# Column-tiled dense groups, row-norm applications on GpSimd, and a later back transposition in a fused attention and token-MLP block

## Chip, cores and metric

The kernel runs on one core of a Trainium2 chip. The metric is device time in microseconds of one execution; the time before is the median of three runs, 292.4 us (292.23 to 293.14). Engines are named as the profile names them: PE is TensorE (PEld its weight loads), DVE VectorE, ACT ScalarE, POOL GpSimd, SP the queue that issues the DMAs.

## What is computed

The reference, cut to what matters (S = 2048 tokens, D = 512, H = 32 heads of 16, window 256, F = 1792):

```python
mod = (silu(c) @ w_mod)            # sa, ca, ga, sb, cb, gb: one row of 512 each
h = layernorm(x) * (1 + ca) + sa
q, k, v = split_heads(h @ wqkv)
scores = q k^T / 4, masked to 0 <= i - j < 256
x = x + ga * (softmax(scores) v) @ wo
h = layernorm(x) * (1 + cb) + sb
h = layernorm(h)                    # the MLP's own norm
u = gelu(h^T @ w1 + b1)             # mixes tokens: contracts S, gives (D, F)
x = x + gb * (u @ w2 + b2)^T
```

The second norm is thus two norms in a row for each token: norm, scale and shift, norm.

## The kernel before

The 2048 tokens are 16 blocks of 128 rows, in four row groups (tg) of four blocks. A short preamble normalises row group 0, makes its first q, k and v, and the modulation rows. Then come two stages.

**The attention stage** is a loop over 80 units: four row groups x four head sets of eight heads (g8) x five kinds of unit (k). In the text, unit u is 20 tg + 5 g8 + k, and "ul" is its number within the row group. Units k = 0, 2, 3, 4 work on "A" scores, k = 1 on "C" scores (the window's diagonal triangles, in 64 x 64 pieces). In each unit the program writes, in this order: the exp of the unit's first score tile (L526), the scores of the next unit (L477 and masks L485, or L504 and L513), in k = 1 and k = 4 the closing of a head set's parity (last value products L557, then the DVE transposition of `po` into `t2`, L583), the matmuls of at most one dense group, the second exp, the queued DVE and POOL work, the evacuation of the dense group, and the value products of the unit before (L537 of A units, L557 of C units).

A dense group is four accumulating matmuls of 128 x 128 weights with 512 columns: v (L250), q or k (L270), a modulation row broadcast (L297), the output projection `wo` (L330) or half of a part of the MLP's first product (L659). `plan(tg)` writes out by hand in which unit each group stands. All use PSUM tile `dn`, which has one buffer; `po`, the accumulator of the value products, also has one; scores have three. Scores run in 32 x 128 and 32 x 64 array tiles, value products in 128 x 32 and 64 x 32, dense groups on the whole 128 x 128 array. A q group's evacuation is the cast to QT (L282), a k group's the cast to ks (L285) on DVE and two masked copies KT (L288) on POOL, v's the cast into VaugT (L261), wo's the residual add into x (L338).

Other work goes through a small planner. `dve` is a list of chains; each chain is a list of steps (function, cost, gap), and `run_dve(u, budget)` lets steps go while their costs fit the unit's budget; after a step its chain rests for `gap` units. The budget comes from a running estimate of DVE's load. Engines run their queues in the order in which the program wrote them, so a step that waits holds what stands behind it on its engine. The chains:

- `norm_rest`: `quotient` (reciprocal zr on DVE, L591; product `merge` on POOL, L592), then `back` (transposition into OTd on DVE, L599), which `wo` reads. It is put ahead of all other chains.
- `ln1_apply`: four normalisations (xn, L218) of the next row group, in units 2 and 3 of a row group.
- `ln23(tb)` for the 12 blocks whose `wo` lies in the loop: `p1` statistics of x on DVE (L608, L610) and rstd on POOL (an add L198 and a pow L202); `p2` application on DVE (L614), then scale and shift on POOL (L625, L626); `p3` statistics of h2 and rstd; `p4` application (L614) into `hb`.

**The MLP stage** contracts `hb` with w1 (L819, L906) and the result with w2 (L926), nearly all on PE; the last four blocks get their output projection (L841) and second norm inside it.

Of the kernel before, what the change touches and what calls it, by code (L numbers as in the profile page):

```python
# [8 lines left out]
DT = mybir.dt  # L9
ACT = mybir.ActivationFunctionType  # L10
ALU = mybir.AluOpType
# [17 lines left out]
def kernel(  # L29
# [25 lines left out]
    dma = nc.sync  # L55

    const = ctx.enter_context(tc.tile_pool(name="const", bufs=1))
    small = ctx.enter_context(tc.tile_pool(name="small", bufs=4))
    xpool = ctx.enter_context(tc.tile_pool(name="xpool", bufs=1))
    xres = [xpool.tile([P, D], DT.bfloat16, name=f"x{t}") for t in range(NT)]  # L60

# [106 lines left out]
    epool = tc.alloc_tile_pool(name="epool", bufs=6)  # L168
    cpool = tc.alloc_tile_pool(name="cpool", bufs=4)
    npool = tc.alloc_tile_pool(name="npool", bufs=2)  # L170
    NG = NT // 4
    QT = [[None] * ND for _ in range(NG)]
    KeT = [[None] * ND for _ in range(NG)]
# [50 lines left out]
    def transpose_group(tg, pair, pool):  # L224
# [18 lines left out]
                )  # L243
        return mms, evac, 1.2

    def v_group(tg, tl, pool, act=False):
        def mms():
            pv = pool.tile([P, D], DT.float32, name="dn")
            for dc in range(ND):
                nc.tensor.matmul(  # L250
                    pv[:], lhsT=h1T[tg][:, dc, tl * P : (tl + 1) * P],
                    rhs=wqkv[:, dc, 2 * D : 3 * D], start=(dc == 0), stop=(dc == ND - 1),
                )
            return pv

        def evac(pv):
            o, i = VaugT[tg][:, tl, :, 0:DH], pv[:].rearrange("p (h d) -> p h d", d=DH)
            if act:
                nc.scalar.activation(out=o, in_=i, func=ACT.Copy)
            else:  # L260
                nc.vector.tensor_copy(out=o, in_=i)  # L261
        return mms, evac, 0.0 if act else 0.7

    def qk_group(tg, g8, kind, pool, act=False):
        col0 = g8 * P + (D if kind == "k" else 0)

        def mms():
            pq = pool.tile([P, 4 * P], DT.float32, name="dn")
            for dc in range(ND):
                nc.tensor.matmul(  # L270
                    pq[:], lhsT=wqkv[:, dc, col0 : col0 + P], rhs=h1T[tg][:, dc, :],
                    start=(dc == 0), stop=(dc == ND - 1),
                )
            return pq
# [18 lines left out]
    def bc_group(v, dst, add1, pool):  # L293
        def mms():
            ps_b = pool.tile([P, D], DT.float32, name="dn")
            for k in range(ND):
                nc.tensor.matmul(  # L297
                    ps_b[:], lhsT=sT_rep[:, k, :], rhs=wmod[:, k, v * D : (v + 1) * D],
                    start=(k == 0), stop=(k == ND - 1),
                )  # L300
            return ps_b

        def evac(ps_b):
            if add1:
                nc.vector.tensor_scalar_add(out=dst[:], in0=ps_b[:], scalar1=1.0)
            else:
                nc.vector.tensor_copy(out=dst[:], in_=ps_b[:])
        return mms, evac, 0.7
# [14 lines left out]
    def wo_group(tb, pool):  # L323
        tg, tl = divmod(tb, 4)

        def mms():
            assert len(folded) == ND
            pa = pool.tile([P, D], DT.float32, name="dn")
            for g in range(ND):
                nc.tensor.matmul(  # L330
                    pa[:], lhsT=OTd[tg][g][:, tl * P : (tl + 1) * P], rhs=wod[:, g, :],
                    start=(g == 0), stop=(g == ND - 1),
                )
            return pa

        def evac(pa):

            nc.vector.tensor_tensor(out=xres[tb][:], in0=pa[:], in1=xres[tb][:], op=ALU.add)  # L338
        return mms, evac, 0.7
# [20 lines left out]
    with tc.manual_schedule():  # L360
# [224 lines left out]
        def norm_rest(tg, g8):  # L585
# [11 lines left out]
            def back():  # L597
                OTd[tg][g8] = opool.tile([P, 4 * P], DT.bfloat16, name=f"OTd{g8}")
                nc.vector.transpose(out=OTd[tg][g8][:], in_=m[:])  # L599
            return [(quotient, 0.4, 1), (back, 0.7, 0)]  # L600


        def ln23(tb):
# [7 lines left out]
                v[key + "r"] = rstd_of(v[key][:, 1:2], 1, "ln2")  # L611

            def apply(out, src, key):
                nc.vector.tensor_scalar(  # L614
                    out=out, in0=src, scalar1=v[key][:, 0:1], scalar2=v[key + "r"][:],
                    op0=ALU.subtract, op1=ALU.mult,
                )
# [2 lines left out]
                stats(xres[tb][:], "m2")  # L620

            def p2():
                v["h2"] = npool.tile([P, D], DT.bfloat16, name="h2")
                apply(v["h2"][:], xres[tb][:], "m2")
                nc.gpsimd.tensor_tensor(out=v["h2"][:], in0=v["h2"][:], in1=bc_cb1[:], op=ALU.mult)  # L625
                nc.gpsimd.tensor_tensor(out=v["h2"][:], in0=v["h2"][:], in1=bc_sb[:], op=ALU.add)  # L626

            def p3():
                stats(v["h2"][:], "m3")

            def p4():
                done.add(tb)
                apply(hb[tb][:], v["h2"][:], "m3")
            return [(p1, 0.9, 2), (p2, 0.45, 2), (p3, 0.9, 2), (p4, 0.45, 0)]

        dve = []

        def add_dve(u, ps):
            dve.append([list(ps), u])

        def run_dve(u, budget):
            spent = 0.0
            for chain in dve:
                while chain[0] and chain[1] <= u and spent + chain[0][0][1] <= budget:
                    f, cost, gap = chain[0].pop(0)
                    f()
                    spent += cost
                    chain[1] = u + gap
# [4 lines left out]
        def part_group(fc, k):  # L653
            def mms():
# [1 line left out]
                if k == 0:  # L656
                    part[fc, "ps"] = ps_dn.tile([P, D], DT.float32, name="dn")
                for sc in range(4 * k, 4 * k + 4):
                    nc.tensor.matmul(  # L659
                        part[fc, "ps"][:], lhsT=w1box["a"][:, sc, fc * P : (fc + 1) * P], rhs=hb[sc][:],  # L660
                        start=(sc == 0), stop=(sc == 7),
                    )
                return part[fc, "ps"]
# [112 lines left out]
            u += 1  # L776

    ps_s.release()
    npool.release()
    cpool.release()  # L780
    epool.release()
# [189 lines left out]
```

## Time and profile before

| | |
|---|---|
| median of 3 runs | 292.4 us |
| the profiled execution | 294.43 us, of it span 292.7 us |
| attention stage (first exp to the first L819) | 16.5 to 194.45 us |
| first MLP product (L819, L906; with the last output projections) | 194.45 to 240.4 us |
| second MLP product and output | 240.4 to 292.7 us |
| busy in 108 to 151 us (43.0 us) | PE 37.14, ACT 38.08, DVE 33.01, POOL 25.75 us |

The stages can be told apart in the chain of waits, since L819, L906 and L926 stand in it as three long pieces. A row of a group tells line, engine, operation, output and input tiles, shape, count; then busy time in all and the mean of one in ns; then the idle time of that engine ahead of these instructions and what ended it. A row of a timeline has the start and the length in us, and in brackets the wait ahead of it and what ended it. The profile's matmuls are pipelined: a single one lasts 0.38 us from start to end, but they start 0.216 us apart, so matmul costs are read from starts.

### The profile page before, as it was taken

What the parts mean: (1) busy time and instruction counts of PE and PEld (TensorE: products, weight loads), DVE (VectorE), ACT (ScalarE), POOL (GpSimd) and SP (SyncE); (2) the same over time, 40 slices, a digit from 0 to 9 for tenths busy, and PEclk for the clock granted to TensorE, in tenths of its full rate; (3) what the DMA queues carried; (4) which work ended last, traced back from release to release, by engine and by line L of the source; (5) the groups of instructions that cost most, each with busy time, mean ns of one, the idle gap of its engine ahead of it and who ended that gap; (6) DMA issues with size and microseconds to landing.
All of it is one profiled execution on the core that took longest, in us unless ns stands there. A gap on an engine that the chain in (4) does not pass through costs nothing.

```text
span 292.7 us, 11229 instructions
## 1 busy us (share of the span) xinstructions
PE 261.8 (89%) x5096; PEld 132.7 (45%) x5096; DVE 170.5 (58%) x358; ACT 170.5 (58%) x192; POOL 99.4 (34%) x163
## 2 busy tenths in 40 slices
PE   7877898998988887898986898999999999999994
PEld 2533454444455454454443454544444444444441
DVE  6464685664778768778667667888902100505253
ACT  7468687897898987989978889923008220000000
POOL 5020423311437634765538556594400000000000
PEclk9799999999999999999979999999999999999999
DMA  6976000069100000000000000089940000012031
GB/s 198 360 238 214 4 2 3 4 226 404 69 4 4 2 4 3 3 4 4 2 4 2 2 4 4 2 287 411 421 203 3 0 0 0 20 55 72 0 110 36
DMA packets 15380, 24.85 MB, mean 85 GB/s; under 512 B 2276, under 2 KB 11492, under 8 KB 15332
## 3 DMA queue, kind: packets, MB, share of 16 engines
q1 hardware_dynamic: 15332, 24.13, 23.1%
q8 instruction: 40, 0.66, 0.9%
q14 instruction: 8, 0.07, 0.1%
HBM read 22.03 MB, written 2.10 MB: 82 GB/s over the span
## 4 chain that ended last, share of the span: by engine, by line
PE 71%; DVE 16%; POOL 6%; ACT 4%; issue 2%; DVEq 0%; POOLq 0%
PE py L926 17%; PE dn L270 8%; PE pu L819 7%; PE pu L906 7%; PE po L537 5%; PE pss L504 4%; PE dn L250 4%; PE pss L477 4%; PE po L557 4%; DVE t L583 4%; PE dn L330 3%; POOL merge L592 3%; PE dn L659 2%; ACT VaugT L381 2%; DVE zr L591 2%
## 5 line engine op out<-in xcount | busy, mean ns | idle before, releaser
L526 ACT ACTIVATE et<-pss 128x1024 bf16<-128x1024 f32 (+1 forms) x160 | 147.1, 980 | 26.3 <-PE pss L485 17.9
L926 PE MATMUL py<-guT,w2r 128*128 128x512 bf16 x224 | 48.5, 379 | 0.0
L270 PE MATMUL dn<-h1T,wqkv 128*128 128x512 bf16 x128 | 33.2, 384 | 4.3 <-DVE h1T L240 1.5
L933 DVE SCALAR_TENSOR_TENSOR o<-py,bFM,bc_gb 128x512 bf16<-128x512 f32 x16 | 11.4, 746 | 43.9 <-PE py L926 43.9
L477 PE MATMUL pss<-QT,KT 32*128 32x192 bf16 (+2 forms) x704 | 26.4, 239 | 8.8 <-ACT et L526 4.7
L926 PEld LDWEIGHTS <-w2r 128*128 128x128 bf16 x224 | 21.9, 98 | 26.4
L592 POOL TENSOR_TENSOR merge<-t,zr 128x512 bf16<-128x512 f32 x16 | 17.0, 1061 | 38.7 <-DVE zr L591 38.7
L583 DVE STREAM_TRANSPOSE t<-po 128x512 f32<-128x512 f32 x32 | 22.9, 717 | 12.3 <-PE po L557 12.3
L537 PE MATMUL po<-et,VaugT 128*32 128x192 bf16 (+2 forms) x704 | 25.2, 244 | 2.4 <-DVE t L583 2.4
L202 POOL TENSOR_TENSOR ln_rstd<-ln_ve,mhalf 128x1 f32<-128x1 f32 (+1 forms) x40 | 24.0, 600 | 3.3
L198 POOL TENSOR_SCALAR ln_ve<-ln_mv 128x1 f32<-128x1 f32 (+1 forms) x40 | 9.8, 244 | 44.5 <-DVE ln_mv L212 21.4
L537 PEld LDWEIGHTS <-VaugT 128*32 128x32 bf16 x704 | 11.6, 95 | 27.4 <-issue 26.7
L477 PEld LDWEIGHTS <-KT 32*128 32x128 bf16 x704 | 11.6, 92 | 19.1 <-issue 13.1
L557 PE MATMUL po<-et,VaugT 64*32 64x64 bf16 x960 | 19.0, 193 | 1.3 <-DVE VaugT L261 1.2
L485 PE MATMUL pss<-mask_q,mask_k 32*128 32x64 bf16 (+1 forms) x736 | 18.3, 197 | 0.0
L250 PE MATMUL dn<-wqkv,h1T 128*128 128x512 bf16 x64 | 17.2, 396 | 0.7 <-DVE ks L285 0.5
L270 PEld LDWEIGHTS <-wqkv 128*128 128x128 bf16 x128 | 10.7, 98 | 15.4 <-issue 4.6
L282 DVE CAST QT<-dn 128x512 bf16<-128x512 f32 x15 | 10.3, 687 | 12.4 <-PE dn L270 8.5
L288 POOL TENSOR_SCALAR KT<-ks,mask_even 128x512 bf16<-128x512 bf16 x14 | 9.7, 694 | 21.1 <-DVE ks L285 21.1
L504 PE MATMUL pss<-QT,KT 32*64 32x64 bf16 x1024 | 14.8, 195 | 1.4 <-issue 1.3
L557 PEld LDWEIGHTS <-VaugT 64*32 64x32 bf16 x960 | 11.0, 92 | 10.6 <-issue 4.8
L485 PEld LDWEIGHTS <-mask_k 32*128 32x128 bf16 x736 | 15.6, 94 | 0.3
(112 smaller groups left out, 358.6 us busy)
## 6 DMA issues: line engine op xcount, KB each, us to landing
w2r<-in_B_w_dram SPq DMA_DIRECT2D x14, 512.0 KB, 9.9
w1a<-in_B_w_dram SPq DMA_DIRECT2D x11, 448.0 KB, 7.7
wmod<-in_w_mod_dram SPq DMA_DIRECT2D x6, 512.0 KB, 4.9
w1b<-in_B_w_dram SPq DMA_DIRECT2D x5, 448.0 KB, 6.5
x<-in_A_x_dram SPq DMA_DIRECT2D x16, 128.0 KB, 2.7
out_dram<-otile SPq DMA_DIRECT2D x16, 128.0 KB, 1.7
wqkv<-in_A_wqkv_dram SPq DMA_DIRECT2D x2, 384.0 KB, 6.2
wqkv<-in_A_wqkv_dram SPq DMA_DIRECT2D x1, 512.0 KB, 6.1
```

The source lines that it names most:

```text
L202: nc.gpsimd.tensor_tensor(out=r[:], in0=ve[:], in1=mhalf[:, 0:n], op=ALU.pow)
L250: nc.tensor.matmul(pv[:], lhsT=h1T[tg][:, dc, tl * P : (tl + 1) * P], rhs=wqkv[:, dc, 2 * D : 3 * D], start=(dc == 0), stop=(dc == ND - 1),)
L270: nc.tensor.matmul(pq[:], lhsT=wqkv[:, dc, col0 : col0 + P], rhs=h1T[tg][:, dc, :], start=(dc == 0), stop=(dc == ND - 1),)
L477: nc.tensor.matmul(pss[j // 2][:, j % 2, c0 : c0 + nq], lhsT=keys(kb, g8, par)[rows[j], k0 : k0 + P], rhs=QT[tg][g8][rows[j], q0 : q0 + nq ...
L485: nc.tensor.matmul(pss[j // 2][:, j % 2, c0 : c0 + 64 * nb].rearrange("p (b q) -> p b q", q=64), lhsT=mask_k[rows[j], P * what : P * what ...
L504: nc.tensor.matmul(pss[a][64 * half : 64 * half + 64, j % 2, c0 : c0 + 64], lhsT=keys(kb, g8, par)[rows[j], k0 : k0 + 64], rhs=QT[tg][g8][ ...
L526: act = nc.scalar.activation(out=et[:, :, 0:n], in_=state.pop((u, a))[:, :, 0:n], func=ACT.Exp, scale=SCORE_SCALE,)
L537: nc.tensor.matmul(state["po"][32 * j : 32 * j + 32, q0 : q0 + nq], lhsT=VaugT[kb // 4][:, kb % 4, 8 * g8 + 2 * j + par, :], rhs=state["e" ...
L557: mm = nc.tensor.matmul(state["po"][32 * j : 32 * j + 32, q0 : q0 + 64], lhsT=VaugT[kb // 4][part64, kb % 4, 8 * g8 + 2 * j + par, :], rhs ...
L583: nc.vector.transpose(out=state["t2"][:, par, :], in_=state["po"][:])
L592: nc.gpsimd.tensor_tensor(out=m[:].rearrange("p (b a d) -> p a b d", a=2, d=DH), in0=t2v[:, :, :, 0:DH], in1=zr[:].to_broadcast([P, 2, 16, ...
L926: nc.tensor.matmul(pys[tl][:], lhsT=w2r[:, fc, tb * P : (tb + 1) * P], rhs=guT[fc][:], start=(fc == 0), stop=(fc == NF - 1),)
```

## The change

It has four parts.

1. Dense groups: each 128 x 128 by 512 matmul of v, q/k, broadcast, `wo` and part groups becomes four matmuls of 128 x 32 weights, each in its own column tile of the array, with the same moving operand, into 32 partitions of the same PSUM tile.
2. `ln23`: both applications (`p2`, `p4`) go from DVE to POOL; `p2` now stands directly behind `p1`, `p4` behind `p3`, with three units between `p2` and `p3`; their planner costs become 0.0.
3. `back` rests two units behind `quotient` instead of one.
4. h2 gets its own pool of three buffers, `small` has six instead of four, and `p2` is let go only while fewer than three rows are between `p2` and `p4`.

```diff
-    small = ctx.enter_context(tc.tile_pool(name="small", bufs=4))
+    small = ctx.enter_context(tc.tile_pool(name="small", bufs=6))
...
+    lnpool = tc.alloc_tile_pool(name="lnpool", bufs=3)
...
+    def dense(out, lhsT, rhs, start, stop):
+
+        for j in range(4):
+            cols = slice(32 * j, 32 * j + 32)
+            nc.tensor.matmul(
+                out[cols, :], lhsT=lhsT[:, cols], rhs=rhs, start=start, stop=stop,
+                tile_position=(0, 32 * j), skip_group_check=True,
+            )
+
     def v_group(tg, tl, pool, act=False):
         def mms():
             pv = pool.tile([P, D], DT.float32, name="dn")
             for dc in range(ND):
-                nc.tensor.matmul(
-                    pv[:], lhsT=h1T[tg][:, dc, tl * P : (tl + 1) * P],
+                dense(
+                    pv, lhsT=h1T[tg][:, dc, tl * P : (tl + 1) * P],
                     rhs=wqkv[:, dc, 2 * D : 3 * D], start=(dc == 0), stop=(dc == ND - 1),
                 )
...
-            return [(quotient, 0.4, 1), (back, 0.7, 0)]
+            return [(quotient, 0.4, 2), (back, 0.7, 0)]
...
             def apply(out, src, key):
-                nc.vector.tensor_scalar(
+                nc.gpsimd.tensor_scalar(
...
             def p2():
-                v["h2"] = npool.tile([P, D], DT.bfloat16, name="h2")
-                apply(v["h2"][:], xres[tb][:], "m2")
-                nc.gpsimd.tensor_tensor(out=v["h2"][:], in0=v["h2"][:], in1=bc_cb1[:], op=ALU.mult)
-                nc.gpsimd.tensor_tensor(out=v["h2"][:], in0=v["h2"][:], in1=bc_sb[:], op=ALU.add)
+                live.add(tb)
+                h2 = v["h2"] = lnpool.tile([P, D], DT.bfloat16, name="h2")
+                apply(h2[:], xres[tb][:], "m2")
+                nc.gpsimd.tensor_tensor(out=h2[:], in0=h2[:], in1=bc_cb1[:], op=ALU.mult)
+                nc.gpsimd.tensor_tensor(out=h2[:], in0=h2[:], in1=bc_sb[:], op=ALU.add)
...
             def p4():
                 done.add(tb)
+                live.discard(tb)
                 apply(hb[tb][:], v["h2"][:], "m3")
-            return [(p1, 0.9, 2), (p2, 0.45, 2), (p3, 0.9, 2), (p4, 0.45, 0)]
+            return [(p1, 0.9, 0), (p2, 0.0, 3, lambda: len(live) < 3), (p3, 0.9, 0), (p4, 0.0, 0)]
...
                 while chain[0] and chain[1] <= u and spent + chain[0][0][1] <= budget:
-                    f, cost, gap = chain[0].pop(0)
+                    if not all(free() for free in chain[0][0][3:]):
+                        break
+                    f, cost, gap = chain[0].pop(0)[:3]
```

The q/k, broadcast, `wo` and part groups call `dense` in the same way as the v group.

## The prediction

> **What bounds the kernel now.** I read the page first, then the groups by form, the chain of waits, the timeline of three stretches, and PE's waits in the attention stage.
>
> ```profile
> span 292.7 us, 11229 instructions
> PE 261.8 (89%) x5096; PEld 132.7 (45%) x5096; DVE 170.5 (58%) x358; ACT 170.5 (58%) x192; POOL 99.4 (34%) x163
> PE 71%; DVE 16%; POOL 6%; ACT 4%; issue 2%; DVEq 0%; POOLq 0%
> ```
>
> ```profile
> 240.38 48.36 PE py L926 x224
> ```
>
> The page's head and its chain by engine; then a row of the chain in order of time (start, length). From 194.45 us on PE runs without a gap (the chain's last rows before the output are PE alone), and the change leaves that half as it is. The attention stage, 16.5 to 194.45 us, is a loop of 80 units. I call T(u) the start of unit u's first exp (L526). ACT starts its two exps 0.92 us apart, so a unit can't be under 1.84 us. Where the chain passes through C scores (k=0) and a dense group it takes 2.30. So PE sets about three units of five, ACT the other two, and stalls come on top. A stall, read from the timeline around unit 44:
>
> ```profile
> 108.85 1.06 POOL L592 TENSOR_TENSOR merge<-t,zr 128x512 bf16<-128x512 f32 x1 [3.19 <-DVE zr L591]
> 109.94 0.71 DVE L599 STREAM_TRANSPOSE OTd<-merge 128x512 bf16<-128x512 bf16 x1 [0.35 <-POOL merge L592]
> 110.58 2.47 DVE L218 TENSOR_SCALAR xn<-x,ln_mv,ln_rstd 128x512 bf16<-128x512 bf16 x4
> 111.10 1.16 POOL L626 TENSOR_TENSOR h<-h,bc_sb 128x512 bf16<-128x512 bf16 x1
> 112.98 0.68 DVE L282 CAST QT<-dn 128x512 bf16<-128x512 f32 x1
> 113.80 0.40 PE L477 MATMUL pss<-QT,KT 32*128 32x256 bf16 x12 [1.46 <-DVE QT L282]
> ```
>
> DVE waits for POOL's merge, everything behind it on DVE is late, the evacuation of QT is last, and PE's next scores start 1.46 us late. So the value of each edit lies in what DVE has to wait for, and POOL is who it waits for.
>
> **Column tiles.** A dense matmul alone costs 48.36/224 = 0.216 us. Behind one, PE starts the next one of its own shape 0.216 us later, but the first L537 0.309 us later (median over the trace): 0.093 us to change the array's shape. Here it shows as four matmuls from 136.28 to 137.24, 0.96 where 4 x 0.216 is 0.86:
>
> ```profile
> 136.28 1.04 PE L330 MATMUL dn<-wod,OTd 128*128 128x512 bf16 x4
> 137.24 0.41 PE L537 MATMUL po<-et,VaugT 128*32 128x256 bf16 x12
> 137.58 0.30 PE L557 MATMUL po<-et,VaugT 64*32 64x64 bf16 x16
> ```
>
> The same lines price the new shape. The 12 L537 matmuls are three pieces of 512 columns in all, in four column tiles, and take 0.34 us with a shape change in them. One after another they would take four times 0.21. So four column tiles stream side by side at full rate, and a dense group keeps its 0.86 us. It becomes L537's shape, so the change behind it goes: 56 groups are followed by L537, 56 x 0.093 = 5.2 us, of which only units with k=0, 1, 4 (and most of row group 0, whose exps are shorter) lie on the path. The change of shape ahead of a dense group stays. 864 extra matmul and load pairs are hidden: in L537 they start 3 to 4 ns apart.
>
> The Trainium skill, TensorE: Matmul & The Clock Gate, Part 3 (The mechanism), says a weight load overlaps running matmuls only where the row group differs; here all four column tiles have the same rows. That would make a rival, priced below. The trace speaks against it: L537 pieces of 64 columns follow each other in 0.03 us with four loads between.
>
> **Applications on POOL.** 24 tensor_scalar leave DVE (L614, 0.46 and 0.41 us, 10.4 in all; DVE is not full, so this counts only where an evacuation stands behind). The trace has no such application on POOL. The nearest row is L288, the same operation and shape with one tensor input, 0.695; the lower bound is the 128x1 tensor_scalar of L198, 0.24, the upper the two-input L625, 1.157. I take 0.70 (one tensor input).
>
> ```profile
> L202 POOL TENSOR_TENSOR ln_rstd<-ln_ve,mhalf 128x1 f32<-128x1 f32 x32 | 18.3, 573 | 2.7
> L592 POOL TENSOR_TENSOR merge<-t,zr 128x512 bf16<-128x512 f32 x16 | 17.0, 1061 | 38.7 <-DVE zr L591 38.7
> L625 POOL TENSOR_TENSOR h<-h,bc_cb 128x512 bf16<-128x512 bf16 x12 | 13.9, 1157 | 4.3 <-DVE h L614 4.3
> L288 POOL TENSOR_SCALAR KT<-ks,mask_even 128x512 bf16<-128x512 bf16 x14 | 9.7, 694 | 21.1 <-DVE ks L285 21.1
> ```
>
> With the 0.08 us between dependent POOL instructions, p1 and p2 of a row are ve 0.30, pow 0.64, apply 0.78, mul 1.24, add 1.11: 4.07 us in one block. p3 and p4 are 0.30 + 0.64 + 0.66 = 1.6. The row takes 5.7 us of POOL against 4.2 before.
>
> **The order.** The planner counts p2 and p4 as 0.0 and lets p1 and p2 go in one unit, so rows come in bursts. Following its budgets unit by unit through the code gives: rows 0, 1 in units 31, 32; 2, 3 in 37, 39; 4, 5, 6 in 49, 50, 51; 7 in 57; 8, 9, 10, 11 in 69, 70, 71, 72. Every merge goes to POOL behind these blocks, and every `back` waits for its merge on DVE, with evacuations (and the transposition of po) behind it; `dn` and `po` have one buffer, so PE then waits too. The second unit of grace (about 2.1 us) is less than one block of 4.07.
>
> At nothing I cost: the larger pools (`small`, `lnpool`; the gate of three rows in flight takes the place of a wait for a buffer); OTd one unit later (`wo` reads it in unit 7 of the next row group, `back` is then in unit 3; were it five units late, `wo` would stand in PE's queue); hb from POOL (rows 0 to 7 are done by unit 60, the parts read them from unit 72; rows 8 to 11 are read after 202 us). No DMA moves.
>
> **The sum**, stage by stage. T is from the exps of the trace. Within a unit I place the steps where the trace has them (the closing's transposition 2.2 to 2.5 us after T, the evacuation of the dense group about 3.4 after), move them later only by the waits that I name, and let each engine take its queue in order with the durations above:
>
> - Units 0 to 31: 20 on-path groups x 0.093 = 1.9, some of it where DVE ends the wait anyway: -1.4.
> - Units 31 to 45 (31.26 us now). POOL starts 4.5 us after T(31) and isn't idle before merge[1,3]: four rows 16.3, three p3+p4 4.8, two merges 2.1, two KT pairs 2.8, ending at 30.5. The three xn now ahead of `back` meet these blocks; an xn beside L626 took 1.31 instead of 0.40. For each the bounds are 0 and 1.16; I take 0.8 in all: merge at 31.3. Behind it on DVE: back 0.71, xn 0.40, QT 0.69, then scores: T(45) at 33.8, +2.5.
> - Units 45 to 69 (54.7 now). merge[2,1] behind rows 4 and 5, and merge[2,2] behind row 6 and three p3+p4, hold DVE by 1.7 us each: +1.1 for units 45 to 61 with the shape changes off. Units 61 to 68 then hold no row work, and their present stalls (1.17 and 1.29 us at L557 and L477, POOL's rows 6 and 7 ahead of an evacuation, and 1.4 in unit 61, where the granted clock was 0.5 for 3.4 us) go: 20.1 to 16.0. Together -3.0.
> - Unit 69 to the MLP (25.3 now, 169.13 to 194.45). POOL starts row 8 at 3.4: four rows 16.3, three p3+p4 4.8, two merges 2.1, so merge[3,2] ends at 26.7. Then back 0.71, transposition of po 0.72, the last value products 1.2: the MLP starts at 29.4, +4.1. Ahead of that p3[11] waits for row 11 until 22.4.
> - MLP: 0. The last `back` lands beside the 2.7 us of L819 that cover it now; without that cover it costs 1 us.
>
> Sum: -1.4 + 2.5 - 3.0 + 4.1 = +2.2 us. The profiled execution took 294.43 (span 292.7 and 1.7 around it), which would become 296.6; the runs' median is 292.4, 2.0 below the profiled one, so 294.6. About 0.3%, 0.9 us, is what a measurement here can tell from no change.
>
> The Trainium skill, SBUF — State Buffer, Who interferes with whom, says DVE in a two-port mode and POOL lock each other out for whole instructions. By that the three xn could cost up to 3 x 1.16 = 3.5, not 0.8, and the time would be 297.3. The 1.31 us xn agrees with it.
>
> **Rivals.**
>
> - *POOL's queue is not waited for (faster).* If POOL gets through its blocks before DVE comes to the merges, stalls go and shape changes are won. The point is the price of the application: some 14 of them lie in the two queues, so at 0.70 - 2.2/14 = 0.54 us the sum is nil, and at 0.24 it is -4.2, 288.2. Spare time in the ACT-bound units that I left out acts the same way. For it: 3.4 us of OTd waits now. Against: L288 never under 0.69. 0.25.
> - *The application costs as much as a two-input operation*: +0.46 x 14 = 6.4, 301. 0.15.
> - *Weight loads not hidden in column tiles*: the loop has 68 dense groups; 68 x 4 chunks each pay an L537 load of 0.095, 26 us, 318. Against: the 0.03 us above. 0.04. The page's rule named above is of this kind.
> - *The shape change does not go away*, so the change doesn't do what it says: 5.2 us on all groups, some 4 on the path, 298.6. 0.06.
> - Forecast: 0.50, of it 0.39 slower, 0.10 same and 0.01 faster.
>
> A stall also reaches the clock: in the sum PE idles about 4.6 us at unit 44, longer than any gap in this stage now, and another slow stretch as in unit 61 would add 1.4.
>
> The range reaches from the faster rival to the dearer application: 288 to 300.5. Faster 0.26 (the first rival, and 0.01), same 0.10, slower 0.64 (0.39 + 0.15 + 0.04 + 0.06).
>
> **What would show it.** Right: dense groups to L537 in 0.87 us; POOL nearly full from units 31 to 44 and 69 to 79; L599 waiting for the merge far over 3.4 us in all; PE's scores of unit 45 waiting 4 us for QT; few stalls in units 61 to 68; the MLP starting later than now relative to T(69). Wrong: an application on POOL under 0.54 us, merges done before DVE asks, or spacing in a column-tiled group over 0.22 us per four.

## The result and the profile after

The changed kernel takes 337.89 us, median of four runs (337.58 to 338.24), against 292.31 us before (290.57 to 293.14): 1.157 times as long, 95% interval 1.1514 to 1.1623. The prediction said slower, but by 2 us; it is slower by 45.6, far outside the range. A few executions of a kernel come out over 1.5% above its fastest one; the times in us below are medians of all runs, the ratios leave these out.

The head of the page, its row of the granted clock, and the chain by engine:

```profile
span 336.0 us, 12954 instructions
PE 278.1 (83%) x5960; PEld 148.4 (44%) x5960; DVE 162.2 (48%) x334; ACT 169.5 (50%) x192; POOL 148.9 (44%) x187
PEclk9779999997998965997966999695799999999999
PE 52%; POOL 28%; DVE 9%; issue 4%; ACT 3%; DMA 2%; SPq 1%; DVEq 0%
```

POOL's share of the chain went from 6% to 28%, and its busy time from 99.4 to 148.9 us. 49.5 us more is nearly three times what 24 applications of 0.70 could add (16.8), and no other step is new on POOL. The clock row holds 5, 6 and 7 where it held 9: between the preamble and the end of the work on PE the core had half the clock for 61.4 us, before for 3.4. The groups say where POOL's time went, and who waits for it (the page's rows for POOL, and DVE's two rows that wait for POOL):

```profile
L624 POOL TENSOR_SCALAR h<-x,ln_mv,ln_rstd 128x512 bf16<-128x512 bf16 x12 | 25.0, 2083 | 1.3
L624 POOL TENSOR_SCALAR hb<-h,ln_mv,ln_rstd 128x512 bf16<-128x512 bf16 x12 | 25.0, 2084 | 1.3
L609 DVE STREAM_TRANSPOSE OTd<-merge 128x512 bf16<-128x512 bf16 x16 | 11.3, 706 | 30.8 <-POOL merge L602 30.8
L618 DVE BATCH_NORM_STATS2 ln_stats<-h 128x6 f32<-128x512 bf16 x12 | 8.2, 683 | 19.6 <-POOL h L637 19.6
```

One application takes 2.08 us on POOL; the sum took 0.70. DVE's wait for the merge grew from 3.4 to 30.8 us, and its wait for h2 at the second statistics from 3.0 to 19.6. The stall ahead of unit 45, the one that the prediction read in the trace of before, is now this (timeline; L251 is any dense group, L609 the transposition into OTd, L292 the cast to QT, L487 scores):

```profile
120.17 2.08 POOL L624 TENSOR_SCALAR h<-x,ln_mv,ln_rstd 128x512 bf16<-128x512 bf16 x1
122.33 1.15 POOL L636 TENSOR_TENSOR h<-h,bc_cb 128x512 bf16<-128x512 bf16 x1
123.56 1.16 POOL L637 TENSOR_TENSOR h<-h,bc_sb 128x512 bf16<-128x512 bf16 x1
123.83 1.90 PE L251 MATMUL dn<-h1T,wqkv 128*32 128x512 bf16 x16
125.68 2.08 POOL L624 TENSOR_SCALAR hb<-h,ln_mv,ln_rstd 128x512 bf16<-128x512 bf16 x1
127.73 1.06 POOL L602 TENSOR_TENSOR merge<-t,zr 128x512 bf16<-128x512 f32 x1
128.82 0.71 DVE L609 STREAM_TRANSPOSE OTd<-merge 128x512 bf16<-128x512 bf16 x1 [5.19 <-POOL merge L602]
129.74 0.68 DVE L292 CAST QT<-dn 128x512 bf16<-128x512 f32 x1
130.57 0.62 PE L487 MATMUL pss<-QT,KT 32*128 32x256 bf16 x12 [4.42 <-DVE QT L292]
```

The merge stands behind a block of row work on POOL, `back` waits 5.19 us for it on DVE, QT stands behind `back`, and PE waits 4.42 us. The dense group of 16 column-tiled matmuls lasts 1.90 us here and 1.05 elsewhere: it ran at half the clock. The same picture stands ahead of units 43, 56, 61 and 76 (7.1, 6.7, 8.3 and 8.1 us from one first exp to the next).

The stages, from the starts of the exps in each profiled execution (difference to the 292.7 us span before, in us; the last column is an experiment of below, in which the application costs what the prediction took):

| stage (its length before) | predicted | after | application at 0.69 us |
|---|---|---|---|
| to the first exp (16.5) | 0 | +0.7 | +0.4 |
| units 0 to 31 (66.6) | -1.4 | +3.9 | +3.5 |
| units 31 to 45 (31.3) | +2.5 | +12.5 | +2.5 |
| units 45 to 61 (34.7) | +1.1 | +11.2 | +4.6 |
| units 61 to 69 (20.1) | -4.1 | -1.6 | -1.7 |
| unit 69 to the MLP (25.3) | +4.1 | +14.7 | +4.1 |
| MLP (98.3) | 0 | +1.9 | +1.7 |
| sum | +2.2 | +43.3 | +15.1 |

### The profile page after: what moved, and what is told of

Its sections match the earlier page's. It is cut to its first block, busy times and chain, and to the rows that moved or that the text cites. A ratio compares the mean times of both kernels' runs of the same rounds, so it can differ in the third digit from the quotient of the medians.

```text
span 336.0 us, 12954 instructions
## 1 busy us (share of the span) xinstructions
PE 278.1 (83%) x5960; PEld 148.4 (44%) x5960; DVE 162.2 (48%) x334; ACT 169.5 (50%) x192; POOL 148.9 (44%) x187
## 4 chain that ended last, share of the span: by engine, by line
PE 52%; POOL 28%; DVE 9%; issue 4%; ACT 3%; DMA 2%; SPq 1%; DVEq 0%
PE py L942 14%; PE dn L251 12%; POOL h L624 7%; PE pu L835 7%; PE pu L922 6%; POOL hb L624 6%; POOL h L636 4%; POOL h L637 4%; POOL ln_rstd L203 3%; PE pss L487 3%; ACT et L536 2%; DVE t L593 2%; PE po L567 2%; PE pss L514 2%; POOL merge L602 2%
## 5 line engine op out<-in xcount | busy, mean ns | idle before, releaser
L251 PE MATMUL dn<-h1T,wqkv 128*32 128x512 bf16 x512 | 37.2, 416 | 5.3 <-DVE QT L292 2.5
L487 PE MATMUL pss<-QT,KT 32*128 32x192 bf16 (+2 forms) x704 | 28.4, 251 | 13.5 <-DVE QT L292 5.8
L547 PE MATMUL po<-et,VaugT 128*32 128x192 bf16 (+2 forms) x704 | 28.5, 264 | 11.3 <-DVE t L593 9.9
L547 PEld LDWEIGHTS <-VaugT 128*32 128x32 bf16 x704 | 19.2, 107 | 28.6 <-issue 18.2
L199 POOL TENSOR_SCALAR ln_ve<-ln_mv 128x1 f32<-128x1 f32 (+1 forms) x40 | 9.8, 245 | 46.1 <-DVE ln_mv L213 24.1
L609 DVE STREAM_TRANSPOSE OTd<-merge 128x512 bf16<-128x512 bf16 x16 | 11.3, 706 | 30.8 <-POOL merge L602 30.8
L203 POOL TENSOR_TENSOR ln_rstd<-ln_ve,mhalf 128x1 f32<-128x1 f32 (+1 forms) x40 | 24.1, 603 | 3.3
L624 POOL TENSOR_SCALAR h<-x,ln_mv,ln_rstd 128x512 bf16<-128x512 bf16 x12 | 25.0, 2083 | 1.3
L624 POOL TENSOR_SCALAR hb<-h,ln_mv,ln_rstd 128x512 bf16<-128x512 bf16 x12 | 25.0, 2084 | 1.3
L487 PEld LDWEIGHTS <-KT 32*128 32x128 bf16 x704 | 12.3, 96 | 25.6 <-issue 21.3
L251 PE MATMUL dn<-wqkv,h1T 128*32 128x512 bf16 x256 | 19.5, 432 | 4.7 <-DVE VaugT L271 4.4
L251 PEld LDWEIGHTS <-wqkv 128*32 128x32 bf16 x512 | 12.4, 101 | 17.5 <-issue 8.5
L495 PE MATMUL pss<-mask_q,mask_k 32*128 32x64 bf16 (+1 forms) x736 | 19.6, 205 | 0.1
L251 PE MATMUL dn<-hb,w1a 128*32 128x512 bf16 x128 | 11.8, 504 | 8.9 <-DVE part L682 8.1
```

Source lines behind the costliest of these rows:

```text
L203: nc.gpsimd.tensor_tensor(out=r[:], in0=ve[:], in1=mhalf[:, 0:n], op=ALU.pow)
L251: nc.tensor.matmul(out[cols, :], lhsT=lhsT[:, cols], rhs=rhs, start=start, stop=stop, tile_position=(0, 32 * j), skip_group_check=True,)
L487: nc.tensor.matmul(pss[j // 2][:, j % 2, c0 : c0 + nq], lhsT=keys(kb, g8, par)[rows[j], k0 : k0 + P], rhs=QT[tg][g8][rows[j], q0 : q0 + nq ...
L547: nc.tensor.matmul(state["po"][32 * j : 32 * j + 32, q0 : q0 + nq], lhsT=VaugT[kb // 4][:, kb % 4, 8 * g8 + 2 * j + par, :], rhs=state["e" ...
L624: nc.gpsimd.tensor_scalar(out=out, in0=src, scalar1=v[key][:, 0:1], scalar2=v[key + "r"][:], op0=ALU.subtract, op1=ALU.mult,)
```

## The experiments

Theory 1 at the start: the mechanism is the predicted one (POOL's queue holds the merge, the merge holds DVE, DVE holds PE), and the price of the application is what was wrong. The rivals: the order, the column tiles, or the clock make the difference. Diffs are abridged, with "..." where code is left out; "before" and "after" name the kernel that is edited. Each ratio is to the kernel before on the same chip in the same job.

**Column tiles alone** (before, with part 1 of the change):

```diff
-                nc.tensor.matmul(pv[:], lhsT=..., rhs=..., start=..., stop=...)
+                dense(pv, lhsT=..., rhs=..., start=..., stop=...)   # and in the four other groups
```

> The kernel before with the dense groups in four column tiles and nothing else. Theory 1 (the shape change behind a dense group is all that this part moves): start of the last dense matmul to the first L547-like value product 0.31 us before, 0.21 to 0.24 here, 56 times; units with k=0 and k=1 at 2.20 instead of 2.30; 2 to 4 us less in all, 288.5 to 290.5. Rival (column tiles themselves cost: 864 more instruction pairs, weight loads, or the granted clock): the units with dense groups get longer and the time goes up, above 294.

296.97 us, ratio 1.0129 (1.0085 to 1.0174): 1.3% slower where 2 to 4 us were to be won, a miss. The gain that was forecast is there: units with k = 0 or 1 take 2.19 to 2.24 instead of 2.30 us, and units 45 to 79 together 73.66 instead of 75.87. But PE stops in the midst of a run of like matmuls, waiting for nothing that the profile shows (timeline, PE):

```profile
69.73 0.29 PE L546 MATMUL po<-et,VaugT 128*32 128x256 bf16 x2
71.76 0.40 PE L546 MATMUL po<-et,VaugT 128*32 128x256 bf16 x10 [1.74 <-issue]
```

A 16 KB instruction fetch had begun at 69.3 us. Units 0 to 31 take 69.95 us instead of 66.62, most of the 3.3 us in the step with this stop and the next one (4.36 and 3.79 us, 3.23 and 2.30 before); from 72.8 us on the clock was halved for 3.4 us.

**Applications back on DVE** (after):

```diff
-                nc.gpsimd.tensor_scalar(
+                nc.vector.tensor_scalar(
```

> The changed kernel with the 24 applications back on DVE; order, gaps, gate and column tiles as changed. Theory 1 (POOL's price of an application, 2.08 us instead of the 0.70 that I took, is the loss): POOL busy falls by 50 us, DVE's waits for merge and h2 fall from 50 us to under 10, time 286 to 293. Rival (the bursts of rows that the zero costs in the planner make are bad whatever the engine): DVE is now over its budget by 0.45 us twice per row, waits stay over 20 us, time over 300.

327.7 us, ratio 1.118 (1.1118 to 1.1241): a miss, with the time and the waits of the rival. The new order writes p2 directly behind p1, so DVE comes to the application before POOL has made rstd (groups, DVE):

```profile
L624 DVE TENSOR_SCALAR hb<-h,ln_mv,ln_rstd 128x512 bf16<-128x512 bf16 x12 | 5.0, 412 | 15.4 <-POOL ln_rstd L203 15.4
L624 DVE TENSOR_SCALAR h<-x,ln_mv,ln_rstd 128x512 bf16<-128x512 bf16 x12 | 4.9, 412 | 16.3 <-POOL ln_rstd L203 16.3
```

The waits for the merge are gone (1.7 us in all), and 31.7 us of others have come. The order belongs to the applications' place; it can't be judged without it. DVE's price for the operation is 0.41 us.

**Applications on POOL alone** (before):

```diff
-                nc.vector.tensor_scalar(
+                nc.gpsimd.tensor_scalar(
```

> The kernel before with the 24 applications on POOL alone: whole-array dense groups, order and gaps of before. Theory 1 (the price of the application decides): POOL does 50 us more, a row's p2 is 4.5 us of POOL, merges and h2 come late, DVE waits for POOL 30 us or more, time 315 to 340, much like the changed kernel. Rival (the order and the bursts do the harm): the rows are spread as before, so under 305.

317.61 us in a single run, as theory 1 expected. DVE waits 24.1 us for h2 and 7.3 for the merge. So the place of the application costs some 24 us without the new order, too.

**Two forms of the operation** (after; p2 subtracts the mean only, p4 is a multiply and an add):

```diff
+    # p2: scalar1=mean, scalar2=1.0, op0=subtract, op1=mult
+    # p4: scalar1=rstd, scalar2=mean, op0=mult, op1=add
```

> The changed kernel with its two POOL applications in two other forms of the same instruction (it leaves out the factor rstd in p2 and swaps factor and shift in p4, so the values are others): p2 subtracts a per-partition value and multiplies by the constant 1.0; p4 multiplies by one per-partition value and adds another. Theory 1 (the second per-partition scalar makes it slow): p2 0.7 us, p4 2.08 us. Theory 2 (the subtraction makes it slow): p2 2.08 us, p4 0.7 us. If each has a share, both between. Either way POOL gets back about 16 us and the time falls to between 300 and 325.

324.65 us in a single run, with the prices of theory 2. The rows (groups, POOL):

```profile
L625 POOL TENSOR_SCALAR h<-x,ln_mv 128x512 bf16<-128x512 bf16 x12 | 24.2, 2016 | 1.0
L630 POOL TENSOR_SCALAR hb<-h,ln_rstd,ln_mv 128x512 bf16<-128x512 bf16 x12 | 9.2, 762 | 1.3
```

The price hangs on the pair of operations: subtract and multiply 2.02, multiply and add 0.76, at equal shapes and with two per-partition scalars in the cheap one.

**Multiply and add** (after; x times rstd plus a 128x1 shift):

```diff
+                nc.gpsimd.tensor_scalar(out=shift, in0=mean, scalar1=rstd, scalar2=-1.0, op0=mult, op1=mult)
-                    scalar1=mean, scalar2=rstd, op0=ALU.subtract, op1=ALU.mult,
+                    scalar1=rstd, scalar2=shift, op0=ALU.mult, op1=ALU.add,
```

> The changed kernel with its 24 POOL applications computed as x times rstd plus (minus mean times rstd), which is the form that took 0.76 us, and one more 128x1 instruction for the shift (0.3 us). This is the prediction's own case with 0.38 to 0.40 us more per application. Theory 1 (the price of the application was the only large error): by the queues of the prediction 301, and some 4 to 6 us more if column tiles cost what they cost alone: 300 to 307; DVE's waits for merge and h2 under 15 us in all; half-clock stretches under 10 us. Rival (the bursts do harm whatever the price): over 315.

320.08 us, ratio 1.0877 (1.0794 to 1.0959): 18 us less than the changed kernel, but 13 over the expected range: a miss. An application is 0.77 us now (groups, POOL), and the shift adds 0.27 to each, so this isn't the price of the forecast yet. DVE still waits 28.9 us for the merge and h2, where under 15 was expected.

```profile
L629 POOL TENSOR_SCALAR h<-x,ln_rstd,ln_shift 128x512 bf16<-128x512 bf16 x12 | 9.2, 767 | 1.3
```

**The same without column tiles:**

```diff
-        for j in range(4): ...                 # four column tiles
+        nc.tensor.matmul(out[:], lhsT=lhsT, rhs=rhs, start=start, stop=stop)
```

> The same with the dense groups on the whole array as before, so the change without its column tiles and with the cheap form. Theory 1 (tiles cost, by stalls in PE's instruction stream, more than the shape changes save): 2 to 6 us less than with the tiles, 297 to 303. Rival (tiles are worth their shape changes here, where PE has more work packed): 3 to 5 us more than with the tiles.

315.18 us, ratio 1.0705 (1.0625 to 1.0785). The difference is what theory 1 expected, though both times lie far above its ranges: the tiles cost 5 us here by the medians. Units 0 to 31 take 67.1 instead of 70.4 us, the later stages agree within 0.5.

**Multiply and add in the order of before** (before, whole array; the edit of "Multiply and add"):

> The kernel before with the applications on POOL in the cheap form, order and gaps of before, whole-array dense groups. A row's p2 is then 3.5 us of POOL instead of 2.4 and DVE has 10 us less to do. Theory 1 (price and order were the harm, not the engine): 290 to 297, DVE's waits for h2 and merge 6 to 14 us. Rival (any application on POOL delays merges and h2 enough to cost PE): over 300.

311.14 us, ratio 1.0543 (1.0427 to 1.0658): the rival. With 24 times 1.04 us more work POOL holds DVE in the old order as well (15.7 us of waits for h2 in the profiled execution, which took 314.98 us).

**Two halves** (before, each dense matmul cut into two of 256 columns on the whole array, so 288 more pairs and no new shape):

```diff
+        for j in range(2):
+            cols = slice(256 * j, 256 * j + 256)
+            nc.tensor.matmul(out[:, cols], lhsT=lhsT, rhs=rhs[:, cols], ...)
```

> The kernel before with each dense matmul cut into two of 256 columns on the whole array: 288 more pairs of load and matmul (a third of what column tiles add), the same array shape, the same PE time within 5 ns per pair. Theory 1 (what column tiles cost is PE running out of instructions, with idle time that ends with nothing the profile shows, some 2.4 us behind the start of an instruction fetch): such stalls grow from 1.7 us by 1 to 3 us, 43 fetches instead of 40, time up by 1 to 3 us. Rival (it is the column tiles' shape): no more such stalls than before, time within 1 us.

299.45 us, ratio 1.0184 (1.0099 to 1.0269). It costs as much as the column tiles and more than the 1 to 3 us expected; two stops for which the profile names no releaser, 4.0 us together, stand at its scores (L512). So the cost comes without the column tiles' shape. It doesn't go by the number of instructions either: this is a third of the added pairs and two more 16 KB fetches (42 against 40; the kernel with tiles has 46).

**PE's waits filled** (after; 137 matmuls of zero weights, so that PE is busy while it waits):

```diff
+    FILL_SCORES = {27: 8, 45: 18}; FILL_GROUP = {32: 4, 37: 9, 41: 18, 54: 11, 74: 18, 78: 15}; FILL_VALUES = {59: 26, 78: 10}
+    nc.tensor.matmul(tile_[:, 1, :], lhsT=zero_weights, rhs=wqkv[:, 0, 0:512], ...)
```

> The changed kernel, with matmuls of zero weights (128x128 by 512 columns, added to a score tile that is not being used by ACT yet) written at the ten places where PE idled over 1 us after unit 26: 137 of them, each place filled to about 0.85 to 0.9 of its idle time in the changed kernel's trace (for instance 18 before the scores of unit 45, 26 before the value products of unit 58). DVE and POOL keep their work, order and waits. Theory 1 (the clock adds to each stall: a stretch of 3.41 us in which PE idles for about 1.6 us or more is followed by one at half the clock): the half-clock stretches behind these places go, of 58 us in all less than 20 stay, and the time falls from 337.9 to 318 to 330 although PE has 30 us more to do; the long steps themselves stay (43 from 42, 45 from 44, 61 from 60 each still over 5 us), since POOL sets them. Rival (POOL's queue alone sets the time, the clock costs only PE time that is waited out anyway): 336 to 341.

334.1 us, ratio 1.1326 (1.1242 to 1.141). The clock came back, the waits on DVE did not change (the page's clock row, then DVE's waits with total, number and longest):

```profile
PEclk9999999999999799989999999999799999999999
```

```profile
DVE OTd L613 <- POOL merge L606: 30.3, 8, 6.3
DVE ln_stats L622 <- POOL h L641: 21.7, 6, 6.0
```

10.2 us at half the clock instead of 61.4, and only 4 us won by the medians, 7 by the ratios. The expectation missed; the rival is nearer. The added matmuls are 137 x 0.216 = 29.6 us of work on PE, which may cost some time themselves, so this is the least that the clock was worth. Where POOL sets the pace, a slower PE mostly uses up what it would have waited.

**The same filling with multiply and add:**

> The same filling in the kernel with the applications as x times rstd plus shift on POOL at 0.77 us (320.1 us, half clock for 34 us): 89 matmuls of zero weights at eleven places. Theory 1: half clock for less than 14 us, time 308 to 316; what is left over 297 is then the queue's waits and the instruction stalls of the column tiles. Rival (the clock costs nothing): 319 to 323.

316.13 us, ratio 1.0661 (1.0583 to 1.0738): just over theory 1's range, and not the rival. Half the clock for 6.8 us; 4 us won by the medians, 6 by the ratios.

**Column tiles, shifted by half a fetch** (64 one-column matmuls in the preamble of the kernel with tiles alone):

> The kernel before with column tiles alone, and 64 more one-column matmuls (128 instructions, half of one 16 KB instruction fetch) in the preamble. Theory 1 (some of PE's stalls that nothing in the profile ends are waits for instructions, and their place follows from where a fetch falls): the stalls of the unshifted kernel (at units 23, 24 and 42 to 45 among them, ending 2.3 to 3.0 us after a fetch began) are gone from these places and others stand about one to one and a half units earlier or at other units, again ending 2.3 to 3.0 us after the start of a fetch; time 294 to 300. Rival (the stalls belong to the code around them, such as 64x32 value products ahead of mask products): they stay in the same units.

303.58 us in a single run, over the expected range. The stops are at other places and longer (4.0 us at the scores of unit 26, in the step from 26 to 27, which takes 8.14 us); units 0 to 31 take 74.7 us. They end 2.3 to 2.6 us after a fetch began, as theory 1 said. Their place settles less: every kernel here whose w1a loads are not spread has such a stop between 64 and 80 us, and that is when the 11 loads of w1a run.

**Scale and shift on DVE** (before):

```diff
-                apply(h2, x, "m2"); nc.gpsimd.tensor_tensor(h2 * bc_cb1); nc.gpsimd.tensor_tensor(h2 + bc_sb)
+                nc.vector.scalar_tensor_tensor(h2 = (x - mean) * bc_cb1)
+                nc.vector.scalar_tensor_tensor(h2 = h2 * rstd + bc_sb)
```

> The kernel before with each row's three steps (application on DVE, scale and shift on POOL) replaced by two on DVE: (x minus mean) times scale, then times rstd plus shift. POOL loses 24 two-input operations (27.7 us), DVE gains one operation a row and longer ones (10 to 14 us). Theory 1 (stalls come from POOL's queue): DVE's wait for the merge falls under 1.5 us in all, PE's waits at the scores of units 45 and 65 and at the value products of 59 and 62 get shorter, and no half clock stays after unit 10: 287 to 291. Rival (DVE becomes what the evacuations wait for): 292 to 297.

310.8 us, ratio 1.0466 (1.0389 to 1.0542): the rival, and dearer than it said. DVE's wait for the merge falls to 2.4 us, but evacuations now stand behind 2 us of row work on DVE itself (timeline, DVE):

```profile
99.79 0.65 DVE L624 SCALAR_TENSOR_TENSOR h<-x,ln_mv,bc_cb 128x512 bf16<-128x512 bf16 x1
100.55 1.36 DVE L628 SCALAR_TENSOR_TENSOR h<-h,ln_rstd,bc_sb 128x512 bf16<-128x512 bf16 x1
101.83 0.68 DVE L282 CAST QT<-dn 128x512 bf16<-128x512 f32 x1
```

The dense group of unit 37 waited 2.1 us for a buffer just then. In this kernel row work costs on either engine, wherever it lies in one block ahead of an evacuation.

**A bare multiply** (after; one operation on POOL):

```diff
+                nc.gpsimd.tensor_scalar(out=out, in0=src, scalar1=rstd, scalar2=None, op0=ALU.mult)
```

> The changed kernel with each application on POOL as a bare multiplication by rstd, one instruction of about 0.69 us: exactly the price that the prediction took. It leaves out the subtraction of the mean. Theory 1 (the walk through the queues was right and only the price wrong): the sum's +2.2 with the column tiles at what they were measured to cost in units 0 to 31 (+3.4 instead of -1.4) gives +7, 299 to 303; units 31 to 45 in 33 to 35 us. Rival (the walk missed waits too, above all DVE's for h2 at the statistics): 308 to 315, units 31 to 45 in over 36 us, and DVE's wait for h over 6 us in all.

327.05 us, ratio 1.1069 (1.0995 to 1.1143). Its price was not the 0.69 us that was meant:

```profile
L624 POOL TENSOR_SCALAR h<-x,ln_rstd 128x512 bf16<-128x512 bf16 x12 | 19.0, 1582 | 1.2
```

A multiply without an add takes more than twice as long as one with it (0.69 to 0.77 us), so this run gives a third price and doesn't test the walk.

**Statistics three units later** (after):

```diff
-            return [(p1, 0.9, 0), (p2, 0.0, 3, ...), ...
+            return [(p1, 0.9, 0), (p2, 0.0, 6, ...), ...
```

> The changed kernel (application at 2.08 us) with a rest of six units instead of three between a row's scale and shift and its second statistics, so that DVE comes to the statistics after POOL has made h2. Theory 1 (DVE's wait for h2 there, 19.6 us, is on the path): that wait falls under 5 us and the time to 322 to 332. Rival (POOL's work sets the time, and the wait goes over to the merges): the wait for the merge grows from 30.8 to over 38 us and the time stays at 334 to 341.

327.63 us, ratio 1.1118 (1.1055 to 1.118): as theory 1 expected. DVE's two waits for POOL (groups, DVE):

```profile
L609 DVE STREAM_TRANSPOSE OTd<-merge 128x512 bf16<-128x512 bf16 x16 | 11.3, 706 | 31.5 <-POOL merge L602 31.5
L618 DVE BATCH_NORM_STATS2 ln_stats<-h 128x6 f32<-128x512 bf16 x12 | 7.9, 658 | 0.0
```

So 10 of the 45 us (13 by the ratios) came by the wait at the statistics. The merges' wait stayed, and a price of 2.08 is still in it.

**Loads of w1a spread**, with and without column tiles (before; one load in every second unit, behind that unit's exp):

```diff
-            sc = next(w1box.get("sc", iter(())), None)
+            sc = next(w1box.get("sc", iter(())), None) if u % 2 else None
+                tc.add_manual_dep(load, exp_of_this_unit, ...)
```

> The kernel before with column tiles alone, and the 11 loads of w1a (448 KB each) let go one in every second unit from 23 to 43 (each behind the exp of its unit) instead of in one burst at 60 to 80 us. Theory 1 (PE waits there for instructions that are fetched late because of the burst): the stalls at the value and score products of units 23 to 26 and the half clock behind them go, units 0 to 31 take 65 to 67 us instead of 69.95, and the time is 288 to 293. Rival (the tiles' own cost, by more instructions, whatever else is loaded): units 0 to 31 stay at 69 to 71 us, time 295 to 298, perhaps with the stalls at other units.

> The kernel before, whole array, with the same spreading of the loads of w1a. Theory 1: unit 26 (3.23 us, a stall of 1.3 that nothing in the profile ends) comes down to 2.3; time 290 to 292.5. Rival (the burst costs it nothing): no change within 0.5%. If the loads' waits on the exps cost something themselves, both spread kernels show it.

With tiles 293.57 us, ratio 0.9975 (0.9943 to 1.0006); without, 292.28 us, ratio 0.9953 (0.9919 to 0.9987). In both, units 23 to 27 run without a stop. Without tiles the step to unit 26 falls from 3.23 to 2.31 us. The tiles' cost falls from 1.3% to 0.2%: most of it hung on the burst of loads, which fits instructions that came late while the loads ran. The rest is stops elsewhere (the steps to units 7 and 42 took 4.92 and 4.70 us), so the expected 65 to 67 us for units 0 to 31 were missed by 0.7. The second kernel is faster than the one before by 0.5%, which its interval just separates from none.

**The price of the forecast** (after; the form of the KT copies):

```diff
+                    scalar1=rstd, scalar2=0.0, op0=ALU.mult, op1=ALU.add,
```

> The changed kernel with each application on POOL as x times rstd plus 0.0, the form of the KT copies, which take 0.69 us: now exactly the price of the prediction, with no further step. It leaves out the subtraction of the mean. Theory 1 (price and column tiles were wrong, the walk through the queues was right): +2.2 with the tiles at the +3.4 measured in units 0 to 31 instead of -1.4 gives +7, 299 to 303. Rival (the walk is wrong too; from 337.9 at 2.08, 327.05 at 1.58 and 320.1 at 0.77 and a step of 0.27, a line gives 313 to 317): 311 to 318, units 31 to 45 in 35.5 to 38 us, and DVE's waits for merge and h together over 15 us.

308.73 us, ratio 1.0497 (1.0426 to 1.0567): 6 us over theory 1, 2 under the rival, so neither range holds it. Units 31 to 45 take 33.77 us, where the walk had 33.8; DVE's waits are 21.0 us together. Its stall at unit 45 (timeline), and DVE's waits:

```profile
112.28 0.69 POOL L624 TENSOR_SCALAR h<-x,ln_rstd 128x512 bf16<-128x512 bf16 x1
117.07 1.05 POOL L602 TENSOR_TENSOR merge<-t,zr 128x512 bf16<-128x512 f32 x1
118.16 0.71 DVE L609 STREAM_TRANSPOSE OTd<-merge 128x512 bf16<-128x512 bf16 x1 [2.25 <-POOL merge L602]
119.91 0.61 PE L487 MATMUL pss<-QT,KT 32*128 32x256 bf16 x12 [3.72 <-DVE QT L292]
```

```profile
L609 DVE STREAM_TRANSPOSE OTd<-merge 128x512 bf16<-128x512 bf16 x16 | 11.3, 705 | 12.4 <-POOL merge L602 12.4
L618 DVE BATCH_NORM_STATS2 ln_stats<-h 128x6 f32<-128x512 bf16 x12 | 8.1, 676 | 8.6 <-POOL h L636 8.6
```

**Column tiles from unit 45 on, loads spread** (before):

```diff
+            if u == 45: tiled.append(u)        # dense() takes the whole array until then
```

> The kernel before with the loads of w1a spread (292.28 us) and column tiles only in the dense groups written from unit 45 on. Theory 1 (the change of shape is a true gain of about 2.2 us in units 45 to 79, the cost of tiles is late instructions, which struck only in units 0 to 45 in the spread kernel with tiles): 289 to 291.5, units 0 to 45 in 97.0 us, units 45 to 79 in 72.9 us instead of 75.07; faster than the kernel before by about 1%. Rival (late instructions follow the tiles into the later units): 291.5 to 295, with a stall of over 1 us in units 45 to 79 that no releaser ends.

292.93 us, ratio 0.9998 (0.9958 to 1.0039): the rival by its time, though no stop in units 45 to 79 is as long as it said. Units 45 to 79 take 74.5 us, 0.5 less than in the spread kernel without tiles (75.07); two stops with no releaser at mask products (129.1 and 162.8 us, 1.1 us together, 2.6 and 2.4 us after a fetch began) take part of what the shape gives. Units 0 to 45, still on the whole array, take 98.0 us instead of 97.0: in the step to unit 34 PE waited 1.2 us for DVE, and the clock was then halved. So the time says less about the tiles than units 45 to 79 do.

## Why the prediction was wrong, step by step

**The application's price: the step that failed.** The prediction took 0.70 us "one tensor input", with 0.24 and 1.157 as bounds; it is 2.08. The row chosen as nearest, L288, multiplies and adds 0.0; the application subtracts and multiplies. What the runs show for a 128x512 bf16 tensor_scalar on POOL:

| operations | us | kernel's ratio, order and tiles of after |
|---|---|---|
| multiply, add 0.0 | 0.69 | 1.0497 |
| multiply, add per-partition | 0.77 (and 0.27 for the shift) | 1.0877 |
| multiply alone | 1.58 | 1.1069 |
| subtract, multiply by 1.0 | 2.02 | |
| subtract, multiply | 2.08 | 1.1569 |

From 0.69 to 2.08 POOL gains 24 x 1.39 = 33.4 us of work, and the span 28.2 (336.0 against 307.8), nearly all of it in the three stages in which POOL is busy for over 80% of the time at 2.08 (units 31 to 61, and unit 69 to the MLP). That is most of the miss of 41.1. The two queues in which the prediction counted 14 applications grew by 10.0 and 10.5 us, close to 14 x 1.38 = 19.3; units 45 to 61, which it left out of that count, grew by 6.6. The rival of the dearer application saw the direction, but its 1.157 was taken for an upper end with no row of that operation on POOL; it was none. By the Trainium skill, GPSIMD Engine Reference, 4.1 (Engine selection), one-input work on GpSimd is roughly at line rate; these rows differ by a factor of three among themselves, and the measurement decides.

**The walk through the queues: right where it was drawn in full.** At its own price it gave units 31 to 45 +2.5 us and +2.5 was measured, unit 69 to the MLP +4.1 and +4.1, and PE's wait for QT 4 us, where 3.72 stood. It put the merge's end at 31.3 us after T(31); it ended at 31.1. Behind unit 69 it put merge[3,2]'s end at 26.7 us and the start of the MLP at 29.4; they came at 26.9 and 29.4. In units 61 to 68 the stalls that it saw going did go, in the changed kernel and at 0.69 us, except that the step to unit 62 ran at half the clock (3.78 and 3.75 us).

**Column tiles: right on the shape, wrong on "hidden".** A dense group is left in 0.87 us where the old one took 0.97 (medians, at the full clock). One of them (after, timeline):

```profile
137.07 1.05 PE L251 MATMUL dn<-h1T,wqkv 128*32 128x512 bf16 x16
137.98 0.41 PE L547 MATMUL po<-et,VaugT 128*32 128x256 bf16 x12
```

Over the trace the first L547 starts 0.19 to 0.24 us behind the last dense matmul (median 0.205), and not 0.309. The weight loads are hidden, as the trace of before had it. But 864 pairs were costed at nothing by the array's time alone: they are 1728 instructions and six more 16 KB fetches (46 against 40), and PE stops 2.2 to 3.0 us after a fetch began. Units 0 to 31 lost 3.3 to 3.9 us instead of winning 1.4. Two halves on the whole array cost the same, and spreading the loads takes most of it away. That PE waits there for instructions, and the fetch behind the loads, is argued from place and time; the trace doesn't show the wait itself, and the fetch's own packet at 69.3 us took 1.08 us, no longer than others.

**The clock: left out of the sum.** The prediction priced one more slow stretch at 1.4 us and kept it outside. At the forecast's price there were seven more of 3.4 us, and the miss in units 45 to 61, in unit 62 and in the MLP is mostly theirs: the steps to units 46, 47 and 62 took 3.87, 3.78 and 3.75 us at half the clock, and 2.24, 2.19 and 2.19 in other column-tiled kernels where the clock was full (4.8 us in all), and the MLP's start gave 1.7. So the 15.1 us at 0.69 are 2.2 forecast, 4.9 for the tiles (with the half clock behind their stops), some 6.5 for the clock behind the queue's stalls, and 1.5 that stay unexplained. At 2.08 us the clock is worth little more (4 to 7 us at least by the filled kernel), since there POOL sets the pace.

**The statistics.** The sum let p3 wait for h2 only at row 11. DVE waited seven times, 19.6 us; three units more of rest took 10 us off.

**Two sums.** The range's upper end, 300.5, lies under its own rival's 301, and the rival of the weight loads adds its 26 us to 292.4 and not to the forecast of 294.6. Neither bears on the result.

Open: whether part 2 and 3 could pay at 0.69 us without the tiles wasn't tried. Little here points that way: the multiply-and-add form, with its shift, costs 5% in the old order and 7% in the new one without tiles. Why the pairs of operations differ so much on POOL isn't shown either.

## What to carry to other kernels

Take an operation's price on an engine from a row with the same operations in the same order, not only the same shape and number of inputs; where there is none, there is no upper bound either, and a range has to say so. More work on an engine that is "a third busy" costs nearly its full length where that engine is full for the stage and others wait in order behind it. Splitting matmuls isn't free because the array hides it: look for stops of PE shortly after instruction fetches, and at what else the DMA engines carry then.

## What the hardware showed that was not expected

- The clock is decided in windows of 3.41 us on a fixed grid. In every trace the stretches at half the clock are multiples of it, but for one at the span's end. Over the 20 traces here (from the first units to some 30 us into the MLP), a window at full clock with under 0.9 us of idle PE was followed by half clock in none of some 880 cases, 0.9 to 1.6 us in 11 of 196, 1.6 to 2.0 in 27 of 44, over 2.0 in 45 of 45. A window at half clock was followed by another in all 39 cases with 0.6 us or more of idle, and in 21 of 107 with less. The Trainium skill, TensorE: Matmul & The Clock Gate, Part 1 (The HAM clock gate), has the window of 3413 ns, which agrees; its abstract rule of no idle gaps over about 3.4 us is too mild here, where one stop of 1.74 us was enough (column tiles alone). The kernel before halved once behind a window with 0.96 us of idle, which idle time alone doesn't explain.
- PE can stop for up to 4.0 us in the midst of like matmuls, where the profile names no releaser. All such stops of 0.4 us or more in the attention stage, over all traces, end 2.2 to 3.0 us after a 16 KB instruction fetch began; between 60 and 80 us, beside 448 KB loads, they were longest.
- On POOL a multiply with an add of zero takes 0.69 us, without it 1.58.
